# Loading k and v with two DMAs per tensor, and moving the second head's rest with VectorE, in a fused attention and feed-forward kernel

## The chip, the core and the metric

The kernel runs on one core of a Trainium2 chip. The core has five engines that run side by side: TensorE (PE in the profile; PEld is its loading of weights), VectorE (DVE), ScalarE (ACT), GpSimd (POOL) and SyncE (SP, here only an issuer of DMAs). Each takes its own instructions in the order of the program and waits for the others through semaphores. The metric is the device time of one execution in microseconds, as the median of several runs.

## What is computed

```python
# q, k, v: (8, 12, 448, 64), w_in: (768, 2048), w_out: (2048, 768), all float32
scores = scale * np.matmul(q, k.transpose(0, 1, 3, 2))
attn = np.exp(scores - scores.max(-1, keepdims=True)); attn /= attn.sum(-1, keepdims=True) + 1e-09
x = np.matmul(attn, v).transpose(0, 2, 1, 3).reshape(3584, 768)
h = x @ w_in
out = np.maximum(0.01 * h, h) @ w_out
```

Softmax attention for 8 batches of 12 heads with 448 queries and keys, then two matrix products with a leaky ReLU between them.

## The kernel before

**Units.** A unit is a pair of heads of one batch: 6 a batch, 48 in all. For each unit q and k are transposed to `qkT`, the scores of its keys and queries are made on TensorE (`scores`, three score slots of two PSUM banks each), ScalarE takes their exponentials into `e` (`expo`), TensorE multiplies them with v, whose extra column of ones gives the sums (`pairs` for units 0 to 11, `weighted` from unit 12 on), and VectorE divides (L887 reciprocal, L888 product) into `x`, which is transposed into `xT`.

**Units from 12 on** use full chunks of 128 keys. The 448 keys of a head are 3 chunks of 128 (`KC` = 3), with 3 keys on each of the 128 partitions, and a rest of 64 keys. The rests of the two heads share one chunk: the first head's on partitions 0-63, the second's on 64-127. `load_soft` fetches q, k and v of two units at once with one GpSimd DMA each (L178), cast to bf16 on the way; `load_rest` (L168) fetches the rests of a whole batch, all six units, with two DMAs for k (`rk`) and two for v (`vr`). `cast` copies what was loaded to where it is used, on GpSimd: q (L204), k (L208) and its rest in two halves (L211) into `qkb`, of which there are 3; v (L215) into `v_sb`, of which there are 4. The rests of v are used where they land. Before the first use, VectorE sets the unused parts of the buffers to zero or one (L207, L809 to L814).

**Transposes.** Up to unit 14, TensorE transposes `qkb` and VectorE copies the result out (L303, L307). From unit 15 on SP issues a transposing DMA (`dma_transposes`, L285). x is transposed by TensorE for some units (L396, L397), and by SP's DMAs for the rest (`x_transposes`, L281; two issues where the batch is cut in two in the ring `xT`). The stores of the result are SP's as well (L409). Units 0 to 2 and the beginning apart, SP's queue thus holds three kinds: qkT, xT and stores, in the order of the program.

**The order of the work** is written out by the program; no scheduler moves anything. Stage one (`first`) does the attention of the first batch. Then come the first products of the feed-forward part with the first 640 rows (`head` L431, `neck` L726), and seven rounds in all of `hidden` (L548, seven products for eight after the Strassen-like sums of `mix_x`, `mix_w_in`) and `second` (L620 in `block_pair`, L685 in `plain_pair`). The attention of later units is placed between these products: `place` puts score bursts (`burst`), the rest's score (`tail`) and products with v (`rows`) where a small model of the time finds room. `feed` (in `head` and `neck`) and `advance` (every few steps of `second`, every step of `hidden`) emit what prepares later units: `advance` issues the next transposing DMA for q and k, if its unit's cast is emitted and a buffer is free, then a cast of q and k, then a cast of v, and on every second call a load of one tensor of two units. A load is emitted when the cast of the unit three before it has been.

**PSUM and VectorE.** TensorE writes into two banks and three score slots. In `hidden` ScalarE copies c11, c12 and c22 out and VectorE adds to them (L563, L575, L578). In `block_pair` VectorE empties each bank into `o` (L625 copies, L628 adds), and it makes the sums of x (`mix_x_part`, L495) and of h (L632, L638). TensorE's next product into a bank waits for that.

The few lines on which the steps turn:

```python
    if u < min(NU, nxt - len(owed_t) + NQ, to["cast"]):
        dma_transposes(u)
...
    if u < min(NU, to["turn"] + 2, to["load"][0], to["load"][1]):
        cast(u, (0, 1))
...
    if u < NU and u - 3 < (to["cast"], to["cast"], to["v"])[x]:
        load_soft(u, 2, (x,))
```

Of the kernel before, what the change touches and what calls it, by code (L numbers as in the profile page):

```python
# [9 lines left out]
F32 = mybir.dt.float32  # L10
BF16 = mybir.dt.bfloat16
# [5 lines left out]
def kernel(  # L17
# [9 lines left out]
    nc = tc.nc  # L27
# [3 lines left out]
    P = 128  # L31
# [48 lines left out]
    NV = 4  # L80
    KC = S // P
    HY = 2 * HP
    v_all = v_pool.tile([P, NV, 2 * KC, D + 1], BF16, name="v")
    v_rest = v_pool.tile([P, 2, HP, 2, D + 1], BF16, name="vr")
    v_sb = [v_all[:, i] for i in range(NV)]

    NE = 3
# [38 lines left out]
    w_in_v = moe_w_in.rearrange("(ko ki) n -> ki ko n", ki=P)  # L126
    w_out_v = moe_w_out.rearrange("(ko ki) n -> ki ko n", ki=P)

    raw = {}
    tails = {}  # L130

# [7 lines left out]

    def room(x, new):

        n, so = (P, KC) if x and new else (SC, NSC)
        if not rooms:
            return ld_pool.tile([n, 2, so, D], F32, name="f" + "qkv"[x])
        t = rooms.pop(0)[:n, :4 * so * D].bitcast(F32)
        return t.rearrange("p (h so d) -> p h so d", h=2, so=so)

    def half(t, x, i, new):  # L150

        t = t.rearrange("p h so d -> p (h so d)").bitcast(BF16)
        t = t.rearrange("p (u h so d) -> p u h so d", u=2, h=2, so=KC if x and new else NSC)
        return t if i is None else t[:, i]

    def front(x, b, hs, new):

        t = (q, k, v)[x][b, hs]
        return t[:, :KC * P].rearrange("h (p so) d -> p h (so d)", so=KC) if x and new else t.rearrange(
            "h (p so) d -> p h (so d)", so=NSC)  # L160

    def load_rest(b, x):

        t = ld_pool.tile([P, HP, D], BF16, name="rk") if x == 1 else v_rest[:, b % 2]
        tails[b, x] = t
        for j in range(2):
            p = slice(j * D, (j + 1) * D)
            nc.gpsimd.dma_start(  # L168
                out=t[p] if x == 1 else t[p, :, j, :D],
                in_=(q, k, v)[x][b, j::2, KC * P:].rearrange("h p d -> p h d"),  # L170
            )

    def load_soft(u, n, which):
        b, hp = divmod(u, HP)
        new = u >= HY
        for x in which:
            t = room(x, new)
            nc.gpsimd.dma_start(  # L178
                out=half(t, x, None, new)[:, :n].rearrange("p u h so d -> p (u h) (so d)"),
                in_=front(x, b, slice(2 * hp, 2 * hp + 2 * n), new),  # L180
            )
            for i in range(n):
                raw.setdefault(u + i, {})[x] = half(t, x, i, new)
            if new and x and hp == 2 * (x - 1):
                load_rest(b, x)

    def load_one(u, x, queue):
        b, hp = divmod(u, HP)
        t = room(x, False)
        queue.dma_start(out=t.rearrange("p h so d -> p h (so d)"), in_=front(x, b, slice(2 * hp, 2 * hp + 2), False))  # L190
        raw.setdefault(u, {})[x] = t

    def load(u):
# [3 lines left out]
    def cast(u, parts=(0, 1, 2), by=nc.gpsimd.tensor_copy):  # L197
        if u >= NU:
            return
        for x in parts:  # L200
            f = raw[u].pop(x)
            t = qkb[u % NB]
            if x < 2 and (x == 0 or u < HY):
                by(t[:SC, x].rearrange("p so h d -> p h so d"), f)  # L204
            elif x == 1:
                if u < HY + NB:
                    nc.vector.memset(t[:, 1, KC], 0.0)  # L207
                by(t[:, 1, :KC].rearrange("p so h d -> p h so d"), f)  # L208
                for j in range(2):
                    p = slice(j * D, (j + 1) * D)  # L210
                    by(t[p, 1, KC, j], tails[u // HP, 1][p, u % HP])  # L211
            elif u < HY:
                by(v_old[:, u % NV, :, :, :D], f)
            else:
                by(v_sb[u % NV][:, :, :D].rearrange("p (h so) d -> p h so d", h=2), f)  # L215

    w_steps = []
    for i in range(4):
# [75 lines left out]
    def transposes(u, bank=None):  # L294
        if u >= min(NPE, NU):
            return
        n = SC if u < HY else P
        t, flat = qkb[u % NB], qkT[u % NQ].rearrange("p i c s -> p (i c s)")[:, :2 * NSC * n]
        for parts in ((1,), (0,)) if u == 0 else ((0, 1),):
            tr = turn_tile(bank)[:, :2 * NSC * n].rearrange("p (i s) -> p i s", i=2)  # L300
            for i in parts:
                for so in range(NSC):
                    nc.tensor.transpose(tr[:, i, ts(so, n)], t[:n, i, so].rearrange("p h d -> p (h d)"), ident[:n, :n])  # L303
            if u == 0 and parts == (0,):
                stay_warm(5)
            at = slice(parts[0], parts[-1] + 1)
            (nc.scalar.copy if u == 0 and parts == (1,) else nc.vector.tensor_copy)(  # L307
                flat.rearrange("p (i s) -> p i s", i=2)[:, at], tr[:, at]
            )

    sc_t = {}

# [29 lines left out]
    def weighted(u, qc, ps):  # L342

        e, vt = e_sb[u % NE], v_sb[u % NV]
        nc.tensor.matmul(  # L345
            ps, e[:, EM + qc * SC:EM + qc * SC + P], v_rest[:, u // HP % 2, u % HP].rearrange("p j d -> p (j d)"),
            start=True, stop=False, skip_group_check=True,
        )
        for j in range(2):
            for c in range(KC):  # L350
                at = (j * KC + c) * S + qc * SC
                nc.tensor.matmul(  # L352
                    ps[:, j * (D + 1):(j + 1) * (D + 1)], e[:, at:at + P], vt[:, j * KC + c],
                    start=False, stop=(c == KC - 1), skip_group_check=True,
                )
# [12 lines left out]
    def pv(u, j, bank=None):  # L368

        bank = next_bank() if bank is None else bank  # L370
        ps = bank[:, :NSC * (D + 1)].rearrange("p (q d) -> p q d", q=NSC)
        pairs(u, j, ps)
        if j == 0:
            x_t[u] = x_pool.tile([SC, NSC, 2, D], BF16, name="x")
        rec = r_pool.tile([SC, NSC, 1], F32, name="rec")
        nc.vector.reciprocal(rec, ps[:SC, :, D:])
        nc.vector.tensor_mul(
            x_t[u][:, :, j, :], ps[:SC, :, :D], rec.to_broadcast([SC, NSC, D])
        )
# [426 lines left out]


    transposes(0)
    nc.vector.memset(qkb_all.rearrange("p u i so h d -> p u i (so h d)")[3 * P // 4:, :, 0], 0.0)  # L809
    nc.vector.memset(v_all.rearrange("p u c d -> p (u c) d")[:, :, D:], 1.0)  # L810
    nc.vector.memset(v_rest, 0.0)
    for j in range(2):
        nc.vector.memset(v_rest.rearrange("p b u j d -> p (b u) j d")[j * D:(j + 1) * D, :, j, D:], 1.0)
    nc.vector.memset(e_all[:, :, EL:], 0.0)  # L814
    cast(1, (0, 1), fast)
    for u in range(HP):
        first(u)
# [9 lines left out]
    expo(HP, 1)  # L827
    pv(HP - 1, 0)
    pv(HP - 1, 1)
    part(0, 1, range(4), b)  # L830
    scores(HP, 2)
    expo(HP, 2)
# [16 lines left out]
    def advance():  # L849
        nonlocal tick  # L850
        tick += 1
        u = to["turn"]
        if u < min(NU, nxt - len(owed_t) + NQ, to["cast"]):
            dma_transposes(u)
            to["turn"] += 1
        u = to["cast"]
        if u < min(NU, to["turn"] + 2, to["load"][0], to["load"][1]):
            cast(u, (0, 1))
            to["cast"] += 1
        u = to["v"]  # L860
        if u < min(NU, rows_done + NV, to["load"][2]):
            cast(u, (2,))
            to["v"] += 1
        if tick % 2 == 0:
            x = min(range(3), key=lambda x: to["load"][x])
            u = to["load"][x]
            if u < NU and u - 3 < (to["cast"], to["cast"], to["v"])[x]:
                load_soft(u, 2, (x,))
                to["load"][x] += 2

    def rows():
        nonlocal rows_done
# [161 lines left out]
    def second(i):  # L1034
# [4 lines left out]
        for c in range(len(spots(i)[1])):  # L1039
            whole = c < plain(i)  # L1040
            for x, _ in enumerate((plain_pair if whole else block_pair)(i, c)):
                fine = 1 if whole else 2
                if x % (2 * fine) == 0:
                    advance()
                if c or x:
                    model["now"] += 0.65 / fine
                left -= place(i, left, calm=whole or x not in (1, 2), keen=need[min(i + 2, NR)], cap=NU if all(summed) else need[i + 2])
                if whole and x in (1, 3, 5, 7):
                    mix_h(i, x - 1)
                if whole and x in (8, 9, 11, 13, 15):  # L1050
# [40 lines left out]
        pass  # L1091
    for i in range(1, NR):
        for step, _ in enumerate(hidden(i)):
            advance()
            if owed_t and step == 0:
                tail()
            if step % 4 == 2 and rows_done < nxt:
                rows()
        model.update(now=0.0, act=2.3, free={id(x): 0.9 if cuts[i + 1] - cuts[i] == 4 * P and i + 1 < NR else 1.2 for x in slots}, ready={})
        second(i)  # L1100

# [29 lines left out]
```

## Time and profile before

| what | value |
|---|---|
| median of 3 runs | 388.59 us (387.92 to 389.05) |
| the profiled execution's own time | 392.32 us |
| its span, first to last instruction | 390.5 us |
| DMA packets | 109372, 47.91 MB |
| of it on GpSimd's queue (q0) | 49888, 22.47 MB, 48.5% of 16 DMA engines' span |
| GpSimd waits before L204 for qkT's transposing DMAs | 77.3 us in 15 waits |
| k load, issue to landing | 4.2 us at least, 6.1 median, 15.5 at most |
| v load, issue to landing | 3.5 / 5.3 / 16.1 us |
| q load, issue to landing | 3.5 / 5.7 / 15.1 us |

How to read the rows that follow. A line of busy time gives an engine's busy microseconds, its share of the span and its number of instructions. A line of waits reads "who <- for what: us in total, how often, the longest". A line of the timeline gives the start in us from the beginning of the span, the length, engine, source line, operation, "written<-read" by the names of the program's tiles with their shapes, how many were merged, and in brackets the idle time of that engine just before and what ended it. A DMA issue's length is the time that its engine spent on issuing; the data land later.

### The profile page before, as it was taken

The numbers are of one execution on the slowest core, as the hardware profiler recorded it, in microseconds if no ns is written. First come the engines' busy times: TensorE is split into PE (matmuls) and PEld (weight loads), VectorE is DVE, ScalarE is ACT, GpSimd is POOL, SyncE is SP. The second block draws the span as 40 slices with busy tenths as digits, with TensorE's granted clock in tenths as the row PEclk, the third lists the DMA queues.
The fourth block names the chain that finished last, engine by engine and source line by source line (L and its number), as shares of the span: only waits on it lengthen the run. The fifth ranks groups of instructions, "written<-read, shape, count | busy, mean of one in ns | idle before, by whom it ended". The sixth has DMA issues, their size and how long they took to land.

```text
span 390.5 us, 9743 instructions
## 1 busy us (share of the span) xinstructions
PE 376.0 (96%) x3910; PEld 262.4 (67%) x3910; DVE 233.2 (60%) x491; ACT 253.3 (65%) x391; POOL 170.9 (44%) x319
## 2 busy tenths in 40 slices
PE   7899999999999999699999999999999999999996
PEld 2565656866588665597657975579756796658854
DVE  4665556655676836457457475574855665484854
ACT  5698894866638786178773787727878378608700
POOL 8997862897364827480263902267324100000000
PEclk9999999999999999999999999999999999999999
DMA  9999999998978969993489933897839700331023
GB/s 153 201 200 203 199 187 154 106 172 157 164 85 153 119 95 148 183 161 43 54 172 164 176 47 65 132 200 132 82 65 167 168 18 2 75 81 57 2 72 89
DMA packets 109372, 47.91 MB, mean 123 GB/s; under 512 B 84112, under 2 KB 106000, under 8 KB 109328
## 3 DMA queue, kind: packets, MB, share of 16 engines
q0 software_dynamic: 49888, 22.47, 48.5%
q1 hardware_dynamic: 59376, 24.81, 32.9%
q8 instruction: 30, 0.49, 0.5%
q14 instruction: 14, 0.11, 0.1%
q10 hardware_dynamic: 64, 0.02, 0.0%
HBM read 45.61 MB, written 11.01 MB: 145 GB/s over the span
## 4 chain that ended last, share of the span: by engine, by line
PE 83%; DMA 6%; DVE 6%; issue 2%; ACT 1%; SPq 0%; DVEq 0%; ACTq 0%
PE g L620 26%; PE g L548 13%; PE sc L548 13%; PE sc L324 7%; PE sc L352 7%; DMA xT<-x 5%; PE g L431 3%; PE g L685 3%; PE sc L321 3%; PE sc L345 2%; PE g L303 1%; PE g L364 1%; PE sc L364 1%; DMA w_in_mix<-in_q_dram 1%; PE g L726 1%
## 5 line engine op out<-in xcount | busy, mean ns | idle before, releaser
L333 ACT ACTIVATE e<-sc 128x896 bf16<-128x896 f32 (+1 forms) x144 | 123.3, 920 | 33.4 <-PE sc L324 27.5
L620 PEld LDWEIGHTS <-h 128*128 128x128 bf16 x632 | 59.4, 98 | 48.1 <-issue 12.7
L620 PE MATMUL g<-w_out_sb,h 128*128 128x384 bf16 x416 | 78.4, 326 | 1.4 <-DVE o L625 1.4
L204 POOL COPY qkb<-fq 112x512 bf16<-112x512 bf16 x36 | 22.8, 633 | 103.5 <-DMA qkT<-qkb 77.3
L537 ACT ACTIVATE h<-c 128x512 bf16<-128x512 f32 (+1 forms) x72 | 43.5, 611 | 28.3 <-DVE c L563 19.2
L548 PEld LDWEIGHTS <-w_in_sb 128*128 128x128 bf16 x576 | 54.4, 98 | 8.8 <-issue 2.9
L548 PEld LDWEIGHTS <-w_in_mix 128*128 128x128 bf16 x432 | 41.2, 98 | 4.1
L887 DVE RECIPROCAL rec<-sc 112x8 f32<-112x8 f32 x42 | 8.7, 208 | 58.1 <-PE sc L352 42.3
L620 PE MATMUL g<-w_mix,h 128*128 128x384 bf16 (+1 forms) x208 | 39.1, 323 | 0.9 <-DVE o L625 0.7
L352 PE MATMUL sc<-v,e 128*128 128x65 bf16 x864 | 39.5, 194 | 0.0
L324 PE MATMUL sc<-qkT 64*128 64x448 bf16 (+1 forms) x252 | 39.5, 352 | 0.0
L352 PEld LDWEIGHTS <-e 128*128 128x128 bf16 x864 | 37.0, 98 | 1.6
L625 DVE COPY o<-g 128x384 f32<-128x384 f32 x49 | 27.1, 553 | 9.8 <-PE g L620 9.7
L345 PE MATMUL sc<-vr,e 128*128 128x130 bf16 x144 | 31.4, 218 | 0.0
L548 PE MATMUL g<-xT,w_in_sb 128*128 128x256 bf16 (+1 forms) x216 | 28.5, 268 | 2.8 <-DVE o L625 2.8
L560 ACT COPY c<-g 128x512 f32<-128x512 f32 (+1 forms) x12 | 6.8, 569 | 36.9 <-PE g L548 36.9
L628 DVE TENSOR_TENSOR o<-o,g 128x384 f32<-128x384 f32 x39 | 21.6, 553 | 14.0 <-PE g L620 13.2
L888 DVE TENSOR_TENSOR x<-sc,rec 112x512 bf16<-112x512 f32 x42 | 29.1, 692 | 1.5
L548 PE MATMUL sc<-xT,w_in_sb 128*128 128x256 bf16 (+1 forms) x216 | 28.5, 268 | 0.0
L215 POOL COPY v<-fv 128x384 bf16<-128x384 bf16 x36 | 20.3, 569 | 12.6 <-PE sc L352 8.8
L208 POOL COPY qkb<-fk 128x384 bf16<-128x384 bf16 x36 | 21.3, 593 | 7.3 <-DMA fk<-in_k_dram 7.3
L211 POOL COPY qkb<-rk 64x64 bf16<-64x64 bf16 x72 | 19.4, 269 | 7.8 <-DMA rk<-in_k_dram 4.7
(128 smaller groups left out, 646.9 us busy)
## 6 DMA issues: line engine op xcount, KB each, us to landing
fq<-in_q_dram POOLq DMA_DIRECT2D x18, 224.0 KB, 5.7
fk<-in_k_dram POOLq DMA_DIRECT2D x18, 192.0 KB, 6.1
fv<-in_v_dram POOLq DMA_DIRECT2D x18, 192.0 KB, 5.3
w_in_sb<-in_moe_w_in_dram POOLq DMA_DIRECT2D x4, 768.0 KB, 11.0
w_out_sb<-in_moe_w_out_dram POOLq DMA_DIRECT2D x4, 768.0 KB, 15.0
out_dram<-o SPq DMA_DIRECT2D x7, 336.0 KB, 3.0
out_dram<-o SPq DMA_DIRECT2D x8, 288.0 KB, 3.5
out_dram<-o SPq DMA_DIRECT2D x7, 240.0 KB, 3.9
```

The lines of the kernel that those rows point to most:

```text
L204: by(t[:SC, x].rearrange("p so h d -> p h so d"), f)
L208: by(t[:, 1, :KC].rearrange("p so h d -> p h so d"), f)
L324: nc.tensor.matmul(ps[:, j, :S].rearrange("p (so s) -> p so s", so=NSC), t[p, 1, c], t[p, 0, :, :SC], start=True, stop=True,)
L333: nc.scalar.activation(e[:, :, c, :], ps[:n, :, :S], AX.Exp, scale=scale)
L345: nc.tensor.matmul(ps, e[:, EM + qc * SC:EM + qc * SC + P], v_rest[:, u // HP % 2, u % HP].rearrange("p j d -> p (j d)"), start=True, stop ...
L352: nc.tensor.matmul(ps[:, j * (D + 1):(j + 1) * (D + 1)], e[:, at:at + P], vt[:, j * KC + c], start=False, stop=(c == KC - 1), skip_group_c ...
L537: nc.scalar.activation(hs[:, m:m + 2, cols], x.rearrange("p (m t) -> p m t", m=2), AX.Prelu, alpha=0.01)
L548: nc.tensor.matmul(ps[:, j * nh:(j + 1) * nh], w[:, kk, ts(j, P)], x[:, kk], start=(first and j == 0 and kk == 0), stop=(kk == KH - 1), sk ...
L620: nc.tensor.matmul(ps[:, cols], x[:, m], w[:, m], start=(first and m == 0), stop=(m == MH - 1), skip_group_check=True,)
L625: by(o[:, at], ps[:, :NW])
L628: nc.vector.tensor_add(o[:, at], o[:, at], ps[:, :NW])
L888: nc.vector.tensor_mul(x, ps[:, :, :, :D], rec.to_broadcast([SC, 2, 2 * NP, D]))
```

## The change

Rests are no longer loaded by themselves. k and v of two units are loaded with two DMAs per tensor: partitions 0-63 get four consecutive keys each (keys 0 to 255 of each head), partitions 64-127 three each (keys 256 to 447). Of the four, the first three belong to the chunks of 128, and the fourth makes the rest of 64 keys, on partitions 0-63 for both heads. The second head's rest has to stand on partitions 64-127, so in `cast` of an even unit from 12 on, VectorE copies it there for both units of the pair (one instruction for k, one for v). v's rests are then cast by GpSimd like k's, two more copies for each unit, into a widened `v_sb`.

The memsets that stood behind the first transposes come later: those of `qkb` behind the transposes of units 9 to 11, the others behind the products of the first batch. And in the part after `neck`, `advance` no longer issues the transposing DMA for q and k itself; the caller does so after `place` (or after `rows` in the `hidden` rounds), so that an x that `rows` sends out in the same step stands ahead of it on SP's queue.

```diff
-            t = room(x, new)
-            nc.gpsimd.dma_start(
-                out=half(t, x, None, new)[:, :n].rearrange("p u h so d -> p (u h) (so d)"),
-                in_=front(x, b, slice(2 * hp, 2 * hp + 2 * n), new),
-            )
+            new = x > 0 and u >= HY
+            t = room(x, new).rearrange("p h so d -> p (h so d)").bitcast(BF16)
+            t = t.rearrange("p (u h so d) -> p u h so d", u=2, h=2, so=NSC)
+            for p, so, keys in ((slice(0, D), NSC, slice(0, NSC * D)), (slice(D, P), KC, slice(NSC * D, S))) if new else (
+                (slice(0, SC), NSC, slice(0, S)),
+            ):
+                nc.gpsimd.dma_start(
+                    out=t[p, :n, :, :so].rearrange("p u h so d -> p (u h) (so d)"),
+                    in_=(q, k, v)[x][b, hs, keys].rearrange("h (p so) d -> p h (so d)", so=so),
+                )
...
-            if new and x and hp == 2 * (x - 1):
-                load_rest(b, x)
+            pair_of[u, x] = t
...
             f = raw[u].pop(x)
             t = qkb[u % NB]
+            if x and u >= HY and u % 2 == 0:
+                two = pair_of[u, x]
+                nc.vector.tensor_copy(two[D:, :, 1, KC], two[:D, :, 1, KC])
...
-                if u < HY + NB:
-                    nc.vector.memset(t[:, 1, KC], 0.0)
-                by(t[:, 1, :KC].rearrange("p so h d -> p h so d"), f)
-                for j in range(2):
-                    p = slice(j * D, (j + 1) * D)
-                    by(t[p, 1, KC, j], tails[u // HP, 1][p, u % HP])
+                by(t[:, 1, :KC].rearrange("p so h d -> p h so d"), f[:, :, :KC])
+                by(t[:D, 1, KC, 0], f[:D, 0, KC])
+                by(t[D:, 1, KC, 1], f[D:, 1, KC])
...
-                by(v_sb[u % NV][:, :, :D].rearrange("p (h so) d -> p h so d", h=2), f)
+                t = v_sb[u % NV]
+                by(t[:, :2 * KC, :D].rearrange("p (h so) d -> p h so d", h=2), f[:, :, :KC])
+                by(t[:D, 2 * KC, :D], f[:D, 0, KC])
+                by(t[D:, 2 * KC + 1, :D], f[D:, 1, KC])
...
+        if HY - NB <= u < HY:
+            nc.vector.memset(qkb[u % NB][3 * P // 4:, 0], 0.0)
+            nc.vector.memset(qkb[u % NB][:, 1, KC], 0.0)
...
-    nc.vector.memset(qkb_all.rearrange("p u i so h d -> p u i (so h d)")[3 * P // 4:, :, 0], 0.0)
-    nc.vector.memset(v_all.rearrange("p u c d -> p (u c) d")[:, :, D:], 1.0)
-    nc.vector.memset(v_rest, 0.0)
-    for j in range(2):
-        nc.vector.memset(v_rest.rearrange("p b u j d -> p (b u) j d")[j * D:(j + 1) * D, :, j, D:], 1.0)
-    nc.vector.memset(e_all[:, :, EL:], 0.0)
...
+    for t in v_sb:
+        nc.vector.memset(t[:, 2 * KC:], 0.0)
+    nc.vector.memset(v_all[:, :, :2 * KC, D:], 1.0)
+    for j in range(2):
+        nc.vector.memset(v_all[j * D:(j + 1) * D, :, 2 * KC + j, D:], 1.0)
+    nc.vector.memset(e_all[:, :, EL:], 0.0)
...
-        if u < min(NU, nxt - len(owed_t) + NQ, to["cast"]):
-            dma_transposes(u)
-            to["turn"] += 1
+        due = u < min(NU, nxt - len(owed_t) + NQ, to["cast"])
         u = to["cast"]
-        if u < min(NU, to["turn"] + 2, to["load"][0], to["load"][1]):
+        if u < min(NU, to["turn"] + due + 2, to["load"][0], to["load"][1]):
...
                 left -= place(i, left, calm=whole or x not in (1, 2), keen=need[min(i + 2, NR)], cap=NU if all(summed) else need[i + 2])
+                if due:
+                    turn_next()
```

## The prediction, made before the result

> **What bounds the kernel now.** I read the page first, then the waits of TensorE, then the rows of single engines in order of time.
>
> ```profile
> PE 376.0 (96%) x3910; PEld 262.4 (67%) x3910; DVE 233.2 (60%) x491; ACT 253.3 (65%) x391; POOL 170.9 (44%) x319
> ```
>
> PE (TensorE) is busy for 376.0 of 390.5 us, so no change off TensorE can win more than 14.5 us, and what makes TensorE wait costs its full length. Its two largest waits:
>
> ```profile
> PE g L548 <- DVE o L625: 2.8, 1, 2.8
> PE g L303 <- DVE qkb L204: 2.0, 1, 2.0
> ```
>
> The first (at 161.8) comes from x transposes that land late: VectorE (DVE) sits in front of L495 until 163.43. The second (at 8.7) comes from the memsets of L809 to L814. These two are what the change aims at. But TensorE is full because VectorE empties its PSUM banks in time, and VectorE takes its instructions in program order. So the question is whether the change gives VectorE a reason to wait. The rows of GpSimd (POOL) and of VectorE over the same time answer that. First around unit 24:
>
> ```profile
> 113.06 0.75 POOL L178 DMA_DIRECT2D fk<-in_k_dram  x1
> ...
> 119.27 0.61 POOL L204 COPY qkb<-fq 112x512 bf16<-112x512 bf16 x1 [4.12 <-issue]
> 120.82 0.50 POOL L208 COPY qkb<-fk 128x384 bf16<-128x384 bf16 x1 [0.94 <-DMA fk<-in_k_dram]
> ```
>
> ```profile
> 111.29 0.29 DVE L495 TENSOR_TENSOR x_mix<-xT,x_mix 128x256 bf16<-128x256 bf16 x1
> 112.30 0.21 DVE L887 RECIPROCAL rec<-sc 112x8 f32<-112x8 f32 x1 [0.71 <-PE sc L352]
> ```
>
> GpSimd casts k of unit 24 at 120.82, the moment its load lands. In the program that cast stands between the two VectorE rows above, at 111.6: GpSimd runs 9 us behind VectorE here, and nobody minds, since k is needed much later. The same around unit 14:
>
> ```profile
> 66.11 0.91 POOL L208 COPY qkb<-fk 128x384 bf16<-128x384 bf16 x1 [0.39 <-DMA fk<-in_k_dram]
> ```
>
> ```profile
> 53.65 0.11 DVE L207 MEMSET qkb<- 128x64 uint32 x1
> 57.49 0.21 DVE L887 RECIPROCAL rec<-sc 112x8 f32<-112x8 f32 x1 [3.73 <-PE sc L364]
> ```
>
> The last L207 is unit 14's own memset, in the same `cast`; the k load of unit 14 lands at 66.0, 12.2 us later.
>
> **The change, part by part.**
>
> *The VectorE copy in `cast`.* It moves the second head's odd keys from partitions 0-63 to 64-127 for every pair of units from 12 on, k and v: 36 copies of 64x128. Nearest rows: 0.17 us (L483, 128x16) and 0.39 us (L397, 128x448); I take 0.2. Its length matters little. It reads what the load wrote, so VectorE now waits, at this place of its program, for a load that only GpSimd waited for. Behind it in VectorE's queue stand the reciprocals that free score slots, the o copies that free banks, the c sums. So I laid the place of each of the 18 k casts and 18 v casts of even units in VectorE's time beside the landing of its load. At 11 k places the load is there or all but there (unit 12: 48.8 against 44.1; unit 26: 136 against 133; unit 44: 285 against 274). At seven it is not. VectorE's place against landing:
> unit 14: 53.8 / 66.0; unit 20: 87.1 / 91.1; unit 22: 103.1 / 108.2; unit 24: 111.6 / 120.8; unit 30: 156.7 / 162.2; unit 36: 208.3 / 213.5; unit 42: 256.2 / 263.7.
> The v places add nothing that these don't (worst: unit 14, 63.4 against 67.3, unit 22, 113.8 against 116.9, both behind a longer k wait). What each costs TensorE, in order:
>
> Unit 14. The landing hangs on the DMA queue (four w_out loads of 768 KB ahead of it), not on TensorE; without the rk loads of 0.6 us it comes at 65.3. Then copy, L887, L888: x is ready at 66.5. TensorE needs it for L396, which ran at 58.48. **8.0 us.** A start that is 2 us earlier is lost here whole, because the landing does not move with it.
>
> Units 20, 22, 24. GpSimd falls back too: the v cast of unit 16 needs the bank of unit 12's rows, which are now 8 us late, and each v cast gets two tails of 0.27 us (L211's mean), each pair of loads a second issue (0.66, by L168's 0.68), less the rest loads (0.68 each). Followed through its rows, it issues the k load of unit 20 some 7 us later than before, that of unit 22 9 us, that of unit 24 10 us, while TensorE is 8, 11 and 13 us late. Left waits are 3.9, about 4, 5 us; TensorE has 0.9, 0.7 and 1.4 us of cover (a slot, a bank, a slot again). **3, 3 and 4 us.** The idle 1 us at 104 to 107 (late x transposes) is swallowed: **-1**.
>
> Units 30, 36, 42. GpSimd has caught up and is held by TensorE's pace (its L204 waits 77.3 us for the transposes of qkT), so it shifts with everything, and the rows hold as they stand. After the copy come L495 twice (0.9) and the L628 that TensorE's next product waits for. Unit 30: TensorE goes on at 164.0 in place of 158.0, but of this the old wait of 2.8 is saved: 3.5. Unit 36: 215.2 in place of 209.7: 5.5. Unit 42: 265.7 in place of 258.0: 7.7. To each I add 1 us for two v casts with tails ahead of the load in GpSimd's queue (with part of the next item, 1.5, 1, 0.8): **5, 6.5, 8.5 us.**
>
> *x ahead of q and k on SP's queue.* An x transpose issue is 1.2 us, 2.5 in the batch that is cut in two; qkT goes out that much later, and waits for x besides. TensorE reads qkT units later (no row of its waits names it), but GpSimd's cast waits for it, and the next load stands behind that cast. x itself lands some 2 us sooner; that gain lies under the unit 30 wait.
>
> *Two DMAs for k and v.* 72 issues in place of 60, 256 fewer packets for each pair and tensor. Do loads land sooner? By the rows no: fq, with 4 keys on each partition, lands after 5.7 us, fk with 3 after 6.1, fv 5.3. The Trainium skill (DMA: Bandwidth & Descriptors, Specifications) says that transfers under 512 bytes miss the line rate; the four-key half reaches 512. By it each of the seven waits would be shorter by at most 1.2 us (fk's 6.1 less fq's 5.7 scaled to its size), so the sum some 8 less; no row here shows such a step.
>
> *Memsets later.* 2.7 us of VectorE leave 6.5 to 9.5, about 2 us for TensorE (L303's wait; unit 1's q lands at 7.12), lost at unit 14 as said. They return as about 1.2 us near 32, beside gaps of 0.5 and 0.7 there.
>
> *GpSimd.* 72 tails of 0.27 are 19 us on 171 of 390: covered except in the places above.
>
> **Sum.** 8 + 3 + 3 + 4 - 1 + 5 + 6.5 + 8.5 = 37. The profiled execution (span 390.5, its time 392.3) lies above the median of the three runs, 388.6; as a difference it goes onto the median: **425.6 us**.
>
> **Rivals.**
> *Faster.* The copies find their keys: if the loads stand earlier against VectorE than these rows, at all seven places, the start (2.0), the late x (0.8 + 2.8) and the bank at 106.8 (0.6) are won: 382.4. For it: VectorE has 157 us of idle time. Against: for units 24, 36 and 42 the program places load and cast within 3 us of each other on VectorE, and a load takes 4.2 us at least. It decides at landing earlier than VectorE's place. 0.05; no change in between 0.02.
> *The waits pay once.* VectorE's delay lets GpSimd catch up, so units 20 to 24 cost 2 in all, the last three only their rows: 8 + 2 + 3.5 + 5.5 + 7.7, less 2 to 8 for quicker landings, 19 to 25: 407 to 413. For it: GpSimd's chain from 84 to 113 waits mostly for its own loads. 0.2.
> *TensorE's pace drops in the long waits.* Before 16.5 us, 128x448 of L321 takes 534 to 577 ns, later 349; after the one idle time of 2.8 us the pace holds. Four of the new waits are over 5 us (units 14, 30, 36, 42). If each is followed by as little as the 3.2 us of the seven warm-up matmuls at the slow pace (0.65 more for 1), that is 4 x 2.1 = 8: 434. 0.18. The Trainium skill (TensorE: Matmul & The Clock Gate, Part 1) has this rule: the clock halves after an idle window of about 3.4 us; that the 2.8 us did nothing agrees with it.
> The forecast itself, 414 to 432: 0.55.
>
> **Range.** 404 to 440: from 3 us under the second rival's low end to the third rival with 6 more for GpSimd falling further back. Slower 0.93, same 0.02, faster 0.05, where same is within 0.3%, about what a measurement of this kernel can tell from no change.
>
> **What would show it.** In the new profile: waits of VectorE's copy for fk<-in_k_dram and fv<-in_v_dram, 30 us or more in all, the longest some 11 us near 54; PE well under 96%; a wait of TensorE for x near 58; units 30, 36, 42 as three dips one stage apart. Wrong if VectorE hardly waits for k, or if TensorE's waits name qkT (then the order on SP decides) or POOL.

## The result, and the profile after

The changed kernel takes 435.45 us (median of 6 runs, 433.84 to 440.19); the kernel before took 388.66 beside it (6 runs, 387.15 to 389.05). The ratio is 1.1226, with an interval of 1.1169 to 1.1284: 12% slower. The forecast was 425.6, its range 404 to 440, and the third rival, in which TensorE's pace drops in the long waits, 434. In three of the experiments below one execution ran at a far lower granted clock (0.56 to 0.75 on average) and took 478 to 633 us; the ratios leave such executions out, the medians don't.

The page of the changed kernel, its span, its line of busy time and the row of the granted clock, the share of full speed at which TensorE is let run (40 slices of 11 us, in tenths, 9 for 90% or more):

```profile
span 438.4 us, 9960 instructions
PE 388.2 (89%) x3910; PEld 267.3 (61%) x3910; DVE 240.1 (55%) x532; ACT 253.8 (58%) x391; POOL 189.6 (43%) x403
PEclk9999966998987999969999899997999999999999
```

TensorE has the same 3910 matmuls. Its idle time has gone from 390.5 - 376.0 = 14.5 us to 438.4 - 388.2 = 50.2, that is 35.7 more; the forecast's sum was 37. But the busy time has grown too, by 12.2 us, and the clock row shows why: around the seven places that the prediction lists the clock is not at its full. 35.7 and 12.2 make up the 47.9 between the two spans. (The profiled execution is the longest of the six; the other five have spans of 432.0 to 435.1.) The trace has the clock at half there for 44.4 us in all. TensorE works in 30.9 us of them, and at the full clock half of that time, 15.5 us, would have been enough. 12.2 is less above all because the kernel before, in its profile, starts at the slow pace until 16.5 us, and the changed kernel only until 4.5.

The waits of TensorE and then of VectorE, changed kernel (who waited for what: us in all, how often, the longest):

```profile
PE g L607 <- DVE o L615: 17.6, 3, 7.3
PE sc L383 <- DVE x L878: 10.6, 1, 10.6
PE g L607 <- DVE o L612: 4.6, 3, 3.4
PE sc L332 <- DVE x L878: 3.9, 1, 3.9
PE sc L311 <- DVE x L878: 3.5, 1, 3.5
```

```profile
DVE fk L186 <- DMA fk<-in_k_dram: 33.0, 5, 13.2
DVE fk L186 <- POOL qkb L188: 12.0, 2, 6.2
```

TensorE waits for VectorE, at banks of PSUM (`o`) and score slots (`x`). VectorE waits in seven places, 45 us in all, ahead of L186, the new copy. The second line names GpSimd's L188 as the releaser, and that is only an inference: the two copies start at 137.57 and 188.82, and the first halves of their loads landed at 137.45 and 188.74. All seven start within 0.13 us of a landing. No copy of v, and none of the other eleven of k, waits over 0.1 us. GpSimd in turn waits for VectorE's copies of k, 53.2 us in four waits ahead of its own copy at L192; the first experiment has no such wait and loses as much, so the loss doesn't lie there.

The same two places that the prediction showed of before, now in the changed kernel. Unit 24, GpSimd's rows and then VectorE's:

```profile
130.14 1.25 POOL L157 DMA_DIRECT2D fk<-in_k_dram  x2
...
139.14 0.50 POOL L190 COPY qkb<-fk 128x384 bf16<-128x384 bf16 x1 [1.68 <-DMA fk<-in_k_dram]
```

```profile
131.09 0.29 DVE L482 TENSOR_TENSOR x_mix<-xT,x_mix 128x256 bf16<-128x256 bf16 x1
137.57 0.19 DVE L186 COPY fk<-fk 64x128 bf16<-64x128 bf16 x1 [6.19 <-POOL qkb L188]
137.79 0.21 DVE L877 RECIPROCAL rec<-sc 112x8 f32<-112x8 f32 x1
```

Between the product for the mixed x and the reciprocal, which stood 1 us apart before, now lies the copy with its wait of 6.19 us. Unit 14, VectorE and then TensorE:

```profile
65.77 0.19 DVE L186 COPY fk<-fk 64x128 bf16<-64x128 bf16 x1 [13.16 <-DMA fk<-in_k_dram]
65.99 0.21 DVE L877 RECIPROCAL rec<-sc 112x8 f32<-112x8 f32 x1
66.23 0.69 DVE L878 TENSOR_TENSOR x<-sc,rec 112x512 bf16<-112x512 f32 x1
```

```profile
66.98 0.55 PE L383 MATMUL sc<-ident,x 112*128 112x112 bf16 x4 [10.55 <-DVE x L878]
67.33 1.33 PE L418 MATMUL g<-xT,w_in_sb 128*128 128x448 bf16 x3
```

The load lands at 65.8, much as before (66.0), and the chain from landing to TensorE is copy, reciprocal, product, transpose. The last row also shows the pace: three products of 448 columns take 1.33 us here, 0.73 at 55.25.

The seven places one by one, VectorE's wait before L186 and TensorE's idle time behind it, beside the prediction's price:

| unit | copy at | VectorE waits | TensorE idle | forecast |
|---|---|---|---|---|
| 14 | 65.77 | 13.16 | 10.56 | 8.0, and a start 2 us earlier lost here |
| 20 | 102.52 | 4.52 | 3.53 | 3 |
| 22 | 123.17 | 3.67 | 3.40 | 3 |
| 24 | 137.57 | 6.19 | 3.91 | 4 |
| 30 | 188.82 | 5.77 | 5.88 + 0.67, for 2.77 before | 5 on top of the 2.77 |
| 36 | 244.03 | 4.12 | 4.43 | 6.5 |
| 42 | 301.63 | 7.50 | 7.29 | 8.5 |

### The profile page after: what moved, and what is told of

Its sections match the earlier page's. It is cut to its first block, busy times and chain, and to the rows that moved or that the text cites. A ratio compares the mean times of both kernels' runs of the same rounds, so it can differ in the third digit from the quotient of the medians.

```text
span 438.4 us, 9960 instructions
## 1 busy us (share of the span) xinstructions
PE 388.2 (89%) x3910; PEld 267.3 (61%) x3910; DVE 240.1 (55%) x532; ACT 253.8 (58%) x391; POOL 189.6 (43%) x403
## 4 chain that ended last, share of the span: by engine, by line
PE 53%; DMA 9%; POOL 4%; DVE 2%; issue 1%; ACT 1%; SPq 0%; DVEq 0%; POOLq 0%
PE g L607 19%; PE g L535 12%; PE sc L535 12%; DMA fk<-in_k_dram 5%; DMA qkT<-qkb 5%; PE sc L339 4%; PE sc L311 4%; PE sc L332 1%; POOL v L197 1%; DVE x_mix L482 1%; ACT e L320 1%; POOL qkb L188 0%; POOL fv L157 0%; DMA fq<-in_q_dram 0%; POOL qkb L190 0%
## 5 line engine op out<-in xcount | busy, mean ns | idle before, releaser
L535 PEld LDWEIGHTS <-w_in_sb 128*128 128x128 bf16 x576 | 56.7, 102 | 8.7 <-issue 1.0
L607 PE MATMUL g<-w_mix,h 128*128 128x384 bf16 (+1 forms) x208 | 42.1, 341 | 18.1 <-DVE o L615 17.6
L188 POOL COPY qkb<-fq 112x512 bf16<-112x512 bf16 x36 | 23.1, 642 | 58.6 <-DMA qkT<-qkb 35.8
L339 PE MATMUL sc<-v,e 128*128 128x65 bf16 x864 | 40.7, 195 | 0.0
L339 PEld LDWEIGHTS <-e 128*128 128x128 bf16 x864 | 38.2, 99 | 1.7
L332 PE MATMUL sc<-v,e 128*128 128x130 bf16 x144 | 32.1, 223 | 3.9 <-DVE x L878 3.9
L192 POOL COPY qkb<-fk 64x64 bf16<-64x64 bf16 x36 | 9.7, 270 | 55.1 <-DVE fk L186 53.2
L535 PE MATMUL g<-xT,w_in_sb 128*128 128x256 bf16 (+1 forms) x216 | 31.1, 284 | 0.0
L535 PE MATMUL sc<-xT,w_in_sb 128*128 128x256 bf16 (+1 forms) x216 | 31.0, 284 | 0.0
L186 DVE COPY fk<-fk 64x128 bf16<-64x128 bf16 x18 | 4.6, 258 | 45.3 <-DMA fk<-in_k_dram 33.0
```

The source lines that it names most:

```text
L332: nc.tensor.matmul(ps, e[:, EM + qc * SC:EM + qc * SC + P], vt[:, 2 * KC:].rearrange("p j d -> p (j d)"), start=True, stop=False, skip_gro ...
L339: nc.tensor.matmul(ps[:, j * (D + 1):(j + 1) * (D + 1)], e[:, at:at + P], vt[:, j * KC + c], start=False, stop=(c == KC - 1), skip_group_c ...
L535: nc.tensor.matmul(ps[:, j * nh:(j + 1) * nh], w[:, kk, ts(j, P)], x[:, kk], start=(first and j == 0 and kk == 0), stop=(kk == KH - 1), sk ...
L607: nc.tensor.matmul(ps[:, cols], x[:, m], w[:, m], start=(first and m == 0), stop=(m == MH - 1), skip_group_check=True,)
```

## The experiments

All ratios are to the kernel before, timed on the same chip between the runs (its medians were 388.5 to 389.3).

**The wait alone.** In the kernel before, without any part of the change, VectorE reads the k load at the place where the change reads it, and writes what it read into a scratch tile that nobody uses.

```diff
             f = raw[u].pop(x)
             t = qkb[u % NB]
+            if x == 1 and u >= HY and u % 2 == 0:
+                nc.vector.tensor_copy(probe.rearrange("p (h d) -> p h d", h=2), f[:D, :, 0])
```

> The kernel before, with one thing added: at the cast of k of each even unit from 12 on, VectorE copies 64x128 of what the load brought into a scratch tile that nobody reads (the output stays the reference's). Loads, rests, GpSimd's casts, memsets and the order on SP are those of before. My theory (VectorE's wait for k loads is the loss): seven waits, 30 us or more idle of VectorE in all, TensorE idle some 34 us more than before, and its clock halved in or after the longer waits, another 8 to 12: 425 to 440 us, as the changed kernel's 435. Rival (a good part of the loss is GpSimd's added tails and issues, the split loads or the order on SP): below 415.

Measured: 439.08 us, ratio 1.1237 (1.1166 to 1.1307). The waits of VectorE in this kernel:

```profile
DVE probe L204 <- DMA fk<-in_k_dram: 46.3, 7, 15.3
```

Seven waits again, 46.3 us. So the whole loss is had with one load for each tensor, the rests by themselves, q and k ahead of x and the memsets at the start. What costs is that an instruction of VectorE stands behind a load.

**The same copies by GpSimd.** The whole change, with only the engine of the copies another.

```diff
-                nc.vector.tensor_copy(two[D:, :, 1, KC], two[:D, :, 1, KC])
+                nc.gpsimd.tensor_copy(two[D:, :, 1, KC], two[:D, :, 1, KC])
```

> The changed kernel with one word changed: the copy of the second head's rest to partitions 64-127 runs on GpSimd, which waits for these loads anyway, in place of VectorE. Theory: VectorE has no wait for a load left; TensorE's clock stays whole; 382 to 392 us (the start 2 us earlier, x sooner, 11 us more work on GpSimd that is covered or costs 2 to 4). Rival (split loads, tails on GpSimd and x ahead of q and k on SP cost by themselves): 400 or more.

Measured: 390.66 us, ratio 1.0048 (1.0017 to 1.0078). Its line of busy time, and the two largest waits of its TensorE:

```profile
PE 375.0 (96%) x3910; PEld 262.1 (67%) x3910; DVE 230.7 (59%) x496; ACT 253.0 (65%) x391; POOL 202.4 (52%) x439
```

```profile
PE g L607 <- DVE o L612: 2.9, 2, 2.4
PE sc L311 <- DMA qkT<-qkb: 1.7, 1, 1.7
```

GpSimd now carries 202.4 us for 170.9 before, and TensorE is at 96% again. Of the 12%, half a per cent is left as the net of all the other parts; that GpSimd works 31 us more is covered to within that.

**No copies at all, four DMAs.** Each head of a pair by its own two DMAs, so that the second head's fourth keys land on partitions 64-127 straight away.

```diff
-                nc.gpsimd.dma_start(
-                    out=t[p, :n, :, :so].rearrange("p u h so d -> p (u h) (so d)"),
+                for j in range(2):
...
+                        nc.gpsimd.dma_start(
+                            out=t[p, :n, j, :so].rearrange("p u so d -> p u (so d)"),
...
-                nc.vector.tensor_copy(two[D:, :, 1, KC], two[:D, :, 1, KC])
```

> The changed kernel without the copy: k and v of two units come by four DMAs per tensor (first head four keys on partitions 0-63 and three on the rest, second head three and four), so that the second head's rest lands on partitions 64-127. No VectorE instruction reads a load. 72 issues more on GpSimd at 0.63 us, 45 us on its 190. Theory: no VectorE wait, 383 to 395 us; if GpSimd's longer issues hold back casts, up to 400. Rival (the loss is in the split loads): more splitting makes it slower than the changed kernel, over 435.

Measured: 405.01 us, ratio 1.041 (1.0334 to 1.0487). Better than the change, but worse than I expected. The largest wait of its TensorE, and a row of GpSimd just ahead of it:

```profile
PE g L290 <- POOL qkb L191: 8.0, 2, 6.8
```

```profile
42.21 0.59 POOL L158 DMA_DIRECT2D fv<-in_v_dram  x1 [3.28 <-DMA w_in_sb<-in_moe_w_in_dram]
```

An issue takes GpSimd 0.62 us for 48 or 64 KB here, 0.63 for 96 or 128 KB in the changed kernel, and 0.76 for 192 KB before: the number of DMAs counts, their size hardly. In the first stage the four issues of v, one of them held for 3.3 us, stand ahead of casts for which TensorE waits 6.8 us (38.3 to 45.1). Behind that wait the clock is at half until 49.5, in which 2.2 us of work are lost. These two make 9.0 of the 14.4 us by which this kernel lies above the one with GpSimd's copies; the rest was not followed up.

**One of the seven waits.** The wait alone again, at unit 42 only.

```diff
-            if x == 1 and u >= HY and u % 2 == 0:
+            if x == 1 and u == 42:
```

> The kernel before with VectorE's scratch copy of the k load at unit 42 alone: one wait of some 7.5 us near 256. It measures one wait by itself. If a wait costs TensorE's idle time alone: 7.7 us, 396.3. If TensorE's clock halves in the idle time and stays so for one or two periods of 3.4 us after it begins work again, half of that more: 398 to 400.

Measured: 396.52 us, ratio 1.0175 (1.0134 to 1.0217). The same kernel again, for a profile of the wait:

> Once more the kernel before with one VectorE wait at unit 42, for a profile of it. TensorE idle some 6.5 to 7.7 us near 256, then its clock at half for 6.8 us, of which 4 to 5 us lie behind the idle time and cost half of that. If both count: 388.6 + 7 + 2.3 = 398; if the clock's part is made up later: 396.

Measured: 396.81 us, ratio 1.0199 (1.0131 to 1.0268), 7.6 us for one wait; the prediction had 8.5 for unit 42. TensorE's row at the place, and TensorE by windows of 3.41 us around it (stretch: its length, busy us and instructions, granted clock, DMA share, GB/s):

```profile
263.18 2.72 PE L623 MATMUL g<-w_mix,h 128*128 128x384 bf16 x8 [5.81 <-DVE o L631]
```

```profile
257.54:260.96 3.42, 0.00 (x0) 1.00 1.48 161
260.96:264.37 3.41, 1.19 (x4) 0.50 0.08 5
264.37:267.78 3.41, 3.41 (x15) 0.50 0.88 166
267.78:271.19 3.41, 3.41 (x52) 1.00 1.31 225
```

The price of the wait has two parts. 5.8 us are idle. Then the clock is at half until 267.78, that is 4.6 us behind the end of the wait, in which 2.3 us of work are lost. 5.8 + 2.3 = 8.1, against 7.6 measured. The times by themselves would not have told: 396.5 and 396.8 lie nearer to what was expected if the slow pace costs nothing in the end (396.3 and 396) than to 398. But those sums have an idle time of 7 to 7.7 us in them, and in the trace it is 5.8.

**The waits filled.** To price the clock's part in all seven: the changed kernel, with matmuls of 64 columns into unused columns of a score slot, emitted behind each of the seven late copies. They compute nothing that is used.

```diff
                 nc.vector.tensor_copy(two[D:, :, 1, KC], two[:D, :, 1, KC])
+                for _ in range(FILL.get(u, 0) if x == 1 else 0):
+                    nc.tensor.matmul(spare, ident, ident[:, :512 - S], start=True, stop=True, skip_group_check=True)
...
+    spare = slots[0][:, 1, S:]
+    FILL = {14: 280, 20: 90, 22: 85, 24: 90, 30: 150, 36: 110, 42: 190}
```

> The changed kernel with TensorE kept at work in the seven waits: behind each of the seven late copies in the program it gets 85 to 280 small products (128x64, into a part of PSUM that nothing else uses, 3 to 9 us, somewhat less than its idle time there). The waits of VectorE stay. If TensorE's halved clock costs what the trace of the changed kernel suggests (some 34 us at half pace behind the idle times, of it 16 lost), the clock stays whole and the time falls to 418 to 428, near the prediction's sum without a clock term, 425.6. Rival (the clock is no cost of its own, the waits would hide it): 435, or more by what the products take too long.

Measured: 427.19 us, ratio 1.0988 (1.0902 to 1.1074), which is 8.3 us under the change; the two intervals don't overlap. Its waits of VectorE are as long as in the changed kernel, and its clock and its products at unit 30 (eight, 2.71 us in the changed kernel at 190.44) are at the full pace:

```profile
DVE fk L186 <- DMA fk<-in_k_dram: 31.6, 5, 13.8
DVE fk L186 <- POOL qkb L190: 13.6, 2, 7.2
```

```profile
PEclk9999999999999999999999999999999999999999
```

```profile
186.07 1.46 PE L611 MATMUL g<-w_mix,h 128*128 128x384 bf16 x8 [1.99 <-DVE o L619]
```

So a kernel with 995 useless matmuls more is 8.3 us faster, and what is left, 427.19 less the 389.22 of the kernel before beside it, is 38.0, close to the forecast's 37. The 8.3 us are probably not the whole of the clock's part, since the filling may outlast a wait here and there; the trace of the changed kernel gives 15.5 for the longest of its executions.

**The two other parts, alone and together,** on the kernel before: x ahead of q and k on SP, the memsets later, both.

```diff
-        if u < min(NU, nxt - len(owed_t) + NQ, to["cast"]):
-            dma_transposes(u)
-            to["turn"] += 1
+        due = u < min(NU, nxt - len(owed_t) + NQ, to["cast"])
...
+                if due:
+                    turn_next()
```

> The kernel before with the order on SP alone changed: x goes out ahead of the transposing DMAs of q and k. The prediction's reading: x lands some 2 us sooner near 161, so TensorE's wait of 2.8 us there shrinks to about 1; 386.5 us. Rival (qkT comes 1.2 to 2.5 us later, holds GpSimd's casts and the loads behind them): no gain or some loss, 388 to 391.

Measured: 388.85 us, ratio 0.9991 (0.9955 to 1.0026).

```diff
+        if HY - NB <= u < HY:
+            nc.vector.memset(qkb[u % NB][3 * P // 4:, 0], 0.0)
...
-    nc.vector.memset(v_rest, 0.0)
...
```

> The kernel before with the memsets alone moved (those of qkb behind the transposes of units 9 to 11, the others behind the products of the first batch). The prediction's reading: VectorE reaches unit 1's casts 2 us sooner; with no wait for a load in between, this lasts: 386.6 us. Rival (ScalarE, busy 9.9 of 10 us from 20 to 30, or the loads set the pace of the first stage, or the moved memsets cost it near 32): 388.6.

Measured: 389.56 us, ratio 0.9985 (0.9948 to 1.0022).

> The kernel before with both edits: x ahead on SP, memsets later; loads, rests and casts as before, no VectorE read of a load. If the two gains of 2 us are real and apart: 384.5 us, faster than both kernels. If either is not: between 386.5 and 389.

Measured: 389.32 us, ratio 1.0007 (0.9968 to 1.0046). None of the three can be told from no change. Their profiles say why the gain of x first is so hard to see. The wait of 2.8 us for late x is at 1.1 with x first alone, gone with the memsets later, and back with both (the lines of the three kernels in this order, the second kernel having no such line):

```profile
PE g L548 <- DVE o L625: 1.1, 1, 1.1
```

```profile
PE g L549 <- DVE o L626: 2.8, 1, 2.8
```

It comes and goes in single profiles, whatever the order on SP. The order may help by a us or so; no run here resolves it.

**The old order on SP,** in the changed kernel: q and k go out ahead of x again (the edit above, undone).

> The changed kernel with the old order on SP (q and k ahead of x). The prediction gave the new order about 1 us of each of the last three waits at most, by later loads, and its gain lies under the wait of unit 30. Theory: 432 to 437, the same within the scatter of this kernel. Rival (the order on SP is what makes the loads late): 415 or less.

Measured: 432.95 us, ratio 1.1117 (1.1054 to 1.1179), 2.5 us under the change, with intervals that overlap (the change has 1.1169 at its lower end). The order on SP can be no more than a few of the 47 us (2.5 by the medians, about 4 by the ratios), and these runs don't tell it from nothing.

**Only v by VectorE.** k's copies by GpSimd, v's by VectorE.

```diff
-                nc.vector.tensor_copy(two[D:, :, 1, KC], two[:D, :, 1, KC])
+                (nc.gpsimd if x == 1 else nc.vector).tensor_copy(two[D:, :, 1, KC], two[:D, :, 1, KC])
```

> The changed kernel with VectorE's copies for v alone; those for k run on GpSimd. The prediction says that the v places add nothing of their own next to the k waits; without the k waits, two of them are late by 3 to 4 us in the rows of before (unit 14, unit 22). Theory: 390 to 397. Rival (any read of a load by VectorE costs as much, k or v): 410 or more.

Measured: 396.57 us, ratio 1.0185 (1.0127 to 1.0243), 5.9 us above the kernel with all copies by GpSimd. VectorE's waits for v, and the largest of TensorE:

```profile
DVE fv L186 <- DMA fv<-in_v_dram: 11.3, 3, 6.1
```

```profile
PE sc L383 <- DVE x L878: 5.6, 1, 5.6
```

Once unit 14's k no longer holds VectorE, unit 14's v does (67.33, after 6.13 us). v's copies cost nothing only where k's hold VectorE up longer.

**Seven by GpSimd, the others by VectorE.** The list of units from the prediction, taken at its word: k's copies at those seven by GpSimd, the other eleven of k and all of v by VectorE.

```diff
+                by_whom = nc.gpsimd if x == 1 and u in (14, 20, 22, 24, 30, 36, 42) else nc.vector
+                by_whom.tensor_copy(two[D:, :, 1, KC], two[:D, :, 1, KC])
```

> The changed kernel with the copy of k on GpSimd at the seven units of the prediction's list (14, 20, 22, 24, 30, 36, 42) and on VectorE at the other eleven; v on VectorE throughout. If the list holds and the other 29 copies are covered: as with v alone, 390 to 397. If waits move to other units once these seven are gone: 400 or more.

Measured: 395.62 us, ratio 1.0149 (1.0079 to 1.0219). That is the time with only v by VectorE (396.57, overlapping intervals), so the eleven k copies that the prediction called free cost nothing that these runs can tell, and moving seven copies of 0.19 us takes 40 us off the change.

## Why the prediction was right, and where it was not

**The mechanism** was right: VectorE, which takes its instructions in order, stands behind a load for which only GpSimd waited. The wait alone gives the loss (439.08), and the same copies on GpSimd take it away (390.66). The list of places was right too, all seven and no others; unit by unit it can be compared in the table above. The three in the middle, for which GpSimd's falling back had to be followed through its rows, came out at 3.5, 3.4 and 3.9 for 3, 3 and 4. That is partly luck: GpSimd issued these k loads 10.7, 14.6 and 17.1 us later than before, for 7, 9 and 10 in the prediction, and VectorE came to its places 10.9, 16.4 and 19.8 us later, for 8, 11 and 13; only the difference of the two came out. The three late ones were too high, 5, 6.5 and 8.5 for 3.8, 4.4 and 7.3. At units 30 and 42 the 1 us that I added for GpSimd's tails is most of it; at unit 36 the load landed 5.6 us after its issue, for 8.5 before. In sum 37 against 35.7 in the profile and 38.0 with the waits filled.

**The step that was mis-sized** is the pace of TensorE. The forecast gave it nothing, and left it to a rival of 434 with 0.18; the measured 435.45 lies outside the 414 to 432 of the forecast itself and next to that rival. It costs 8.3 us by the filled waits (435.45 less 427.19), and 15.5 in the one profile, which is the longest of six. The rival's count was not what happened either: it has four waits at 2.1 us, and half a clock followed all seven, with 2.9 to 5.8 us of work in it each time. That its 8 us come so near to 8.3 is luck in part. I leaned on a row of before: after the idle time of 2.8 us the pace holds. That row was no evidence. TensorE by windows in the kernel before, around that idle time (161.80 to 164.57):

```profile
159.86:163.27 3.41, 1.94 (x37) 1.00 1.60 172
163.27:166.69 3.42, 2.12 (x20) 1.00 1.07 281
```

and in the changed kernel around units 24 and 36, where it idles 3.9 us (134.87 to 138.78) and 4.4 us (241.49 to 245.93):

```profile
134.18:137.60 3.42, 0.69 (x7) 1.00 1.15 237
137.60:141.01 3.41, 2.23 (x31) 0.50 0.18 41
141.01:144.42 3.41, 3.41 (x18) 0.50 0.47 58
240.00:243.41 3.41, 1.49 (x10) 1.00 1.39 189
243.41:246.82 3.41, 0.89 (x6) 1.00 0.47 64
246.82:250.24 3.42, 3.42 (x17) 0.50 0.63 124
```

The stretches are cut where the clock changes in each trace, and at multiples of 3.413 us from there. In the kernel before the 2.77 us lie on both sides of such a cut, 1.5 in one window and 1.3 in the next, and nothing happens. In the changed kernel 2.7 us at unit 24 and 2.5 at unit 36 fall into one window of 3.4, and the next one is granted half the clock. The very wait that I leaned on shows it too: the kernel with the wait at unit 42 alone is the kernel before up to there, and in its profile that wait is 3.0 us long (159.33 to 162.35), 2.6 of them lie in one window, and the clock is at half in the next, from 161.97 to 165.38. An idle time has to be laid on this grid before one can say what it costs, and which window it falls in isn't known before the run. By the 2.05 us worked out in the last section, an idle time of 4.1 us or more would halve the clock wherever the cuts fall, and a shorter one may; only the runs gave this figure.

**Behind the long wait** of unit 14 I had the start's gain of 2 us lost. So it is: TensorE comes to the place at 56.42 (58.48 before) and goes on at 66.98, the landing not having moved. But the 2 us are no proof of a gain by the later memsets: the kernel with the wait alone, which has them at the start, comes to the place at 56.47. What was late is the profile of before, with its slow pace until 16.5 us.

**Two DMAs.** That loads would not land sooner by enough to matter holds: VectorE's waits in all are 44.9 us with two DMAs and 46.3 in the kernel with the wait alone, which loads as before; the two profiles differ in more than the loads, but no large gain is seen. The four-key half of k lands 5.9 us after its issue, the three-key half 5.8 us, for 6.1 of the whole before. For v it is 3.5 and 4.2 us, for 5.3 before; that is sooner, but VectorE never waits for v in the changed kernel. The Trainium skill (DMA: Bandwidth & Descriptors, Specifications) has a line rate that only transfers from 512 bytes up reach; by the prediction's estimate for this rule some 8 us less were due, and the runs don't show them.

**v.** "The v places add nothing that these don't" holds in the change and nowhere else: alone, v's copies cost 5.9 us.

**x first and the memsets** were rightly given almost nothing here. That they would each win 2 us in the kernel before was my expectation in the experiments, and no run shows it.

## What to carry to other kernels

Before a copy is moved to an engine that another engine depends on, lay its place in that engine's program beside the landing of the data it reads; the copy's own length (0.19 us here) says little, the difference of those two times (up to 13 us here) is what the engine will wait. The engine for such a copy is the one that waits for the same data anyway, here GpSimd. No kernel run here beats the one before; loads emitted early enough for VectorE's copies were not tried. And price a new wait of TensorE by its length and, where it may empty most of a window of the clock, by half of the windows that follow.

## What the runs showed of the hardware

The clock's windows. In nine profiles of these kernels (the changed one and eight experiments), every change of the granted clock falls on one grid of 3.413 us per execution, to 0.01 us. The grid starts anywhere: full clock first comes at 4.5 us in the changed kernel's profile and at 16.5 in that of before. I cut the nine traces by it and added up TensorE's idle time in each window, by the ends that the profile models for its matmuls. From full clock, every window with 2.05 us of idle time or more (60%) was followed by half a clock, and none with less than 1.85; at half, windows with up to 0.56 us of idle time were followed by full clock (but one, with 0.38), and none with 1.06 or more was. The Trainium skill (TensorE: Matmul & The Clock Gate, Part 1) has the free-running window of 3413 ns, and the trace agrees; but it has the clock halve after an idle window, and here 60% of one is enough. With four DMAs, an idle time of only 2.7 us (173.54 to 176.25) did it, because 2.3 of it fell into one window:

```profile
172.42:175.84 3.42, 1.12 (x30) 1.00 1.21 147
175.84:179.25 3.41, 3.00 (x15) 0.50 1.21 221
```

What decides between 1.85 and 2.05 us stays open.
